# An attention, Fourier and feed-forward kernel: batch 0's first copies of the attention values move to VectorE, and three groups of instructions get other predecessors

## The chip, the cores and the metric

The kernel runs on one core of a Trainium2 chip. A core has TensorE (PE, matmuls, with PEld for the weight loads), VectorE (DVE), ScalarE (ACT), GpSimd (POOL) and SyncE (SP), which issues most of the DMA transfers. Each engine works through its own queue in order and waits for the others by semaphores. The metric is the device time of one execution in microseconds (us). The profile is of one execution of its own.

## The reference

For 8 batches, 8 heads, 576 tokens and a head size of 64: attention over keys and values that are averaged over 8 neighbours, then a two-dimensional Fourier transform of which the real part is added, a normalisation, and a feed-forward layer of 512 to 2048 to 512.

```python
k_p = k.reshape(B, H, Sp, pool, D).mean(axis=3)          # Sp = 72
v_p = v.reshape(B, H, Sp, pool, D).mean(axis=3)
scores = scale * np.matmul(q, k_p.transpose(0, 1, 3, 2))
attn = softmax(scores)                                    # exp, sum, divide
x = np.matmul(attn, v_p)                                  # to (B, S, 512)
...
u = x + np.real(np.fft.fft(np.fft.fft(x, axis=1), axis=2))
un = (u - mean(u)) / np.sqrt(var(u) + 1e-06)
out = u + np.maximum(un @ w_ch1, 0.0) @ w_ch2
```

## The kernel before

Everything is kept transposed, channels on the partitions, tokens along the free dimension. A batch's front end (`fe(b)`, a generator that is stepped by the main loop) makes `unh` and `unl`, a high and a low part of the centred activations; the feed-forward layer (`ffn`) multiplies high by high, low by high and high by low, so that three matmuls stand for one in float32. Its loop runs over blocks of 288 or 384 tokens and in each over 8 or 16 steps `f` (128 hidden channels): 12 matmuls into `g`, a Relu on ACT (`hh`), its rest on DVE (`hl`), 12 matmuls into `acc`.

The front end of batch 0 runs alone before the first block; that of batch 1 is interleaved with the first block, those of later batches with later blocks. In `fe`: `prep_k` (sums of keys into `ks`, then `kpb`), `scores` (`psS`, maxima `mx`, exponentials `t`, division on POOL), `transposes` (`psT`, `psV`, `psR` on PE; `ah` and `R` are their copies in SBUF by ACT, `rt` the copy of the columns of `t` that stand beyond 128), and `values(g)` for four pairs of heads, in the order 3, 2, 0, 1: `psX` (`ah` by `wh`, plus `R` by `wlo`), which for g = 3 and 2 is copied into `X` and for g = 0 and 1 added to and subtracted from it on DVE. Then the Fourier transform: `tmpE` and `tmpO` are sums and differences of halves of `X`, each split into a high part (`eh`, `oh`, by ACT) and a low part (`el`, `ol`, by DVE; all four are named `f` in the profile), `xe` a row that is treated apart; `psA` takes `eh`, `el`, `xe`; `psB` takes `oh` and `ol`; `psQ`, `psP` are the second transform; `psM` the mean, `less` (L661) subtracts it, `centre` (L645, L646) makes `unh` on ACT and `unl` on DVE, once for each half of the tokens.

The weights come as float64. `load_w(n)` loads piece n (two pieces, one of each matrix, for a step) into a staging buffer `wst`; `prep_w(n)` turns it into a float32 `wd`: L196 and L198 on ACT, L201 and L202 on DVE; then the cast to the high part (`w1h`, `w2h`, L206, ACT), the low part on POOL (L207), which is written to memory (L208) and loaded again step by step as `w1low`, `w2low`. The preparation of pieces 0 to 10 stands ahead of the first block in the program, that of the others between its steps. A staging buffer is loaded anew when L202 of the piece in it is done.

The order on each engine is made by a scheduler that weighs the whole program. It is bound by data and by `tc.issue_after(x)`, which puts an instruction behind x. Two tables use it for weights: `HOLD` names for each piece what L196 stands behind, `HOLDV` what L201 stands behind; "R" is the last copy of batch 0's `R`, "E" the making of `el`, "X" the first `less` of batch 0, "z" the last `unl` of its first half. Batch 1's DVE work on scores and on sums of values stands behind "z" already. `keep_busy` puts matmuls without a use (`idle` in the profile) into gaps of PE.

Of the kernel before, what the change touches and what calls it, by code (L numbers as in the profile page):

```python
# [22 lines left out]
P = 128  # L23
NPAIR = 4
W2J = 2 * J
# [27 lines left out]
E0, O0, E1, O1 = 0, 1, 2, 3  # L53
# [2 lines left out]
BUSY = {"start": 8, "S3": 3, "S2": 7, "S0": 9, "S1": 4, "T3": 3, "T0": 6, "R": 4, "X": 10, "A": 3, "P": 6, "M": 8}  # L56

HOLD = {2: "R", 3: "R", 4: "R", 5: "R", 6: "B", 7: "B", 8: "B"}
HOLDV = {4: "E", 5: "E", 6: "X", 7: "X", 8: "X"}

EARLY = [4, 6]

# [24 lines left out]
def tile_kernel(ctx: ExitStack, tc: tile.TileContext, qt, kt, vm, vr, w1, w2, cad, cbd, mkd, out):  # L87
    nc = tc.nc
# [92 lines left out]
    def prep_w(n):  # L181
        if n >= len(pieces):
            return
        i, f, c, w, _ = pieces[n]
        cl = slice(c * P, (c + w) * P)
        if wide:
            st = staged.pop(n)
            hi = st[:, :, :, 1]
            halves = st.bitcast(U16)
            d0 = wk.tile([P, DM], I32, tag="w", bufs=7, name="wd")[:, 0:w * P]  # L190
            di = d0.rearrange("p (c m) -> p c m", m=P)
            dh = d0.bitcast(U16).rearrange("p (c m h) -> p c m h", m=P, h=2)
            d0 = d0.bitcast(F32)

            with tc.issue_after(behind[HOLD[n], 0].ins) if n in HOLD else ExitStack():
                nc.scalar.activation(hi.bitcast(F32), hi.bitcast(F32), AF.Copy, scale=REBIAS)  # L196

                nc.scalar.activation(dh[:, :, :, 0], st.bitcast(U8)[:, :, :, 3], AF.Copy, scale=1.0 / 32.0, bias=-15.5 / 32.0)  # L198

            with tc.issue_after(behind[HOLDV[n], 0].ins) if n in HOLDV else ExitStack():  # L200
                nc.vector.tensor_scalar(out=dh[:, :, :, 1], in0=halves[:, :, :, 3], scalar1=0x8000, scalar2=None, op0=ALU.bitwise_and)  # L201
            nc.vector.scalar_tensor_tensor(out=di, in0=hi, scalar=3, in1=di, op0=ALU.logical_shift_left, op1=ALU.bitwise_or)  # L202
        else:
            d0 = staged.pop(n)
        wh = high(i, f)[:, cl]
        nc.scalar.copy(out=wh, in_=d0)  # L206
        nc.gpsimd.tensor_tensor(out=d0, in0=d0, in1=raw(wh), op=ALU.subtract)  # L207
        nc.sync.dma_start(wls[i][:, f, cl], d0)  # L208
        for m in after.get(n, ()):
            load_w(m)  # L210
# [39 lines left out]
    def fe(b):  # L250
# [85 lines left out]
        def scores(gi, i):  # L336
# [10 lines left out]
            for c0, n in ((0, 3), (3, 2)):  # L347
                ps = bank(b, f"psS{b}_{g}_{c0}")
                for c in range(n):
                    r0 = SROW[c0 + c]  # L350
                    mm = nc.tensor.matmul(ps[:, c * W2J:(c + 1) * W2J], lhsT=q[:, r0:r0 + P], rhs=kpb[g % 2], start=True, stop=True)  # L351
                if b == 0 and c0:
                    keep_busy(BUSY[f"S{g}"], mm)
                pv = ps[:, 0:n * W2J].rearrange("p (c h j) -> p c h j", h=2, j=J)
# [74 lines left out]
        def values(g):  # L429
            ah, al = st["a"][g]  # L430
            wh, wl = st["w", g]
            for cl in halves:
                ps = bank(b, f"psX{b}_{g}")[:, 0:HS]
                if b in NAT:
# [5 lines left out]
                if b == 0 and g == 1 and cl.start:  # L440
                    keep_busy(BUSY["X"], last)
                if g == 3:
                    nc.scalar.copy(out=Xb[:, O0, cl], in_=ps)
                    nc.scalar.copy(out=Xb[0:1, E1, cl], in_=ps[0:1])
                elif g == 2:
                    nc.scalar.copy(out=Xb[:, O1, cl], in_=ps)
                    nc.scalar.copy(out=Xb[0:1, O0, cl], in_=ps[0:1])
                    nc.scalar.copy(out=Xb[0:1, O1, cl], in_=Xb[0:1, E1, cl])
                else:
                    e = 2 * g  # L450
                    nc.vector.tensor_tensor(out=Xb[:, e, cl], in0=ps, in1=Xb[:, e + 1, cl], op=ALU.add)
                    nc.vector.tensor_tensor(out=Xb[:, e + 1, cl], in0=ps, in1=Xb[:, e + 1, cl], op=ALU.subtract)
# [114 lines left out]
        for i, m in enumerate(shares):  # L567
            if b:
                channels(i, m, 0)
            ps, _ = channels(i, m, 1)  # L570
            if i < 2:
                parts((AB[i],), ps, 258)
            else:
# [424 lines left out]
```

## Time and profile before

| what | us |
|---|---|
| median of 3 runs | 1086.92 (1086.22 to 1087.01) |
| profiled execution | 1087.56 |
| its span, first to last instruction | 1085.6 |
| PE busy in the span | 1051.1 (97%) |
| DVE, ACT, POOL busy | 615.3, 414.0, 256.0 |

The profiled execution lies 0.64 us above the median, and 1.96 us of it lie outside the span. Times within the profile are counted from the start of the span. A busy PE may still work at half its clock; the granted clock is shown beside it. In a timeline a row may merge several instructions (x4); the figure in brackets is how long the engine stood idle before it, and for what.

### The profile page before, as it was taken

The numbers are of one execution on the slowest core, as the hardware profiler recorded it, in microseconds if no ns is written. First come the engines' busy times: TensorE is split into PE (matmuls) and PEld (weight loads), VectorE is DVE, ScalarE is ACT, GpSimd is POOL, SyncE is SP. The second block draws the span as 40 slices with busy tenths as digits, with TensorE's granted clock in tenths as the row PEclk, the third lists the DMA queues.
The fourth block names the chain that finished last, engine by engine and source line by source line (L and its number), as shares of the span: only waits on it lengthen the run. The fifth ranks groups of instructions, "written<-read, shape, count | busy, mean of one in ns | idle before, by whom it ended". The sixth has DMA issues, their size and how long they took to land.

```text
span 1085.6 us, 17737 instructions
## 1 busy us (share of the span) xinstructions
PE 1051.1 (97%) x6626; PEld 1016.3 (94%) x6626; DVE 615.3 (57%) x1233; ACT 414.0 (38%) x1083; POOL 256.0 (24%) x264
## 2 busy tenths in 40 slices
PE   8878898999999999999999999999999999999998
PEld 7667688999999999999999999999999999999997
DVE  6698877855376455656376455756467434522122
ACT  5868754443244331533243431443324422311110
POOL 6626365211240032311141032300231101300000
PEclk9889999999999999999999999999999999999999
DMA  8859876655345444444444444445435333346563
GB/s 310 257 186 319 282 259 211 201 177 159 113 120 165 131 153 138 128 141 157 136 124 148 133 150 137 139 131 160 140 106 156 97 106 120 116 129 191 163 190 100
DMA packets 91909, 175.80 MB, mean 162 GB/s; under 512 B 10160, under 2 KB 17328, under 8 KB 91568
## 3 DMA queue, kind: packets, MB, share of 16 engines
q1 hardware_dynamic: 91248, 171.71, 51.0%
q0 software_dynamic: 288, 2.66, 0.6%
q8 instruction: 52, 0.85, 0.3%
q10 hardware_dynamic: 288, 0.30, 0.1%
q14 instruction: 33, 0.27, 0.1%
HBM read 156.81 MB, written 17.83 MB: 161 GB/s over the span
## 4 chain that ended last, share of the span: by engine, by line
PE 86%; DVE 5%; ACT 3%; DMA 3%; POOL 1%; issue 1%; SPq 0%; DVEq 0%; POOLq 0%; ACTq 0%
PE g L775 35%; PE acc L759 35%; PE psX L439 3%; PE psS L351 3%; PE psA L558 2%; PE psP L601 2%; PE psB L584 1%; PE psQ L601 1%; PE psT L392 1%; DMA w2l<-wd 1%; POOL wd L207 1%; DMA w1low<-w1l 1%; ACT wd L198 1%; DMA k<-in_kt 1%; PE psR L415 1%
## 5 line engine op out<-in xcount | busy, mean ns | idle before, releaser
L779 ACT ACTIVATE hh<-g 128x384 fp32r<-128x384 f32 (+1 forms) x208 | 96.6, 464 | 338.1 <-PE g L775 318.4
L780 DVE SCALAR_TENSOR_TENSOR hl<-g,hh 128x384 fp32r<-128x384 f32 (+1 forms) x208 | 108.8, 523 | 189.1 <-ACT hh L779 184.2
L759 PE MATMUL acc<-hh,w2h 128*128 128x384 f32 (+1 forms) x832 | 187.2, 327 | 0.9 <-ACT hh L779 0.7
L759 PE MATMUL acc<-hh,w2low 128*128 128x384 f32 (+1 forms) x832 | 187.3, 327 | 0.0
L775 PE MATMUL g<-unh,w1low 128*128 128x384 f32 (+1 forms) x832 | 181.1, 331 | 4.6 <-DMA w1low<-w1l 4.6
L759 PE MATMUL acc<-hl,w2h 128*128 128x384 f32 (+1 forms) x832 | 182.2, 327 | 0.9 <-DVE hl L780 0.8
L775 PE MATMUL g<-unl,w1h 128*128 128x384 f32 (+1 forms) x832 | 178.2, 328 | 3.0 <-DVE unl L646 3.0
L775 PE MATMUL g<-unh,w1h 128*128 128x384 f32 (+1 forms) x832 | 172.4, 326 | 3.1 <-DVE hl L780 2.3
L775 PEld LDWEIGHTS g<-unh,w1low 128*128 128x128 f32 x832 | 140.1, 190 | 7.8 <-DMA w1low<-w1l 5.9
L759 PEld LDWEIGHTS acc<-hh,w2h 128*128 128x128 f32 x832 | 142.9, 188 | 2.7 <-ACT hh L779 1.8
L775 PEld LDWEIGHTS g<-unh,w1h 128*128 128x128 f32 x832 | 139.7, 189 | 4.6 <-DVE hl L780 2.8
L775 PEld LDWEIGHTS g<-unl,w1h 128*128 128x128 f32 x832 | 139.9, 189 | 4.3 <-DVE unl L646 3.7
L759 PEld LDWEIGHTS acc<-hh,w2low 128*128 128x128 f32 x832 | 143.1, 188 | 0.4 <-issue 0.4
L759 PEld LDWEIGHTS acc<-hl,w2h 128*128 128x128 f32 x832 | 141.6, 189 | 2.0 <-DVE hl L780 1.8
L371 POOL TENSOR_TENSOR t<-t,sm 128x720 f32<-128x720 f32 x32 | 47.4, 1482 | 267.4 <-DVE sm L370 247.2
L286 POOL TENSOR_TENSOR k<-k 128x288 f32<-128x288 f32 (+1 forms) x56 | 37.5, 670 | 84.7 <-DMA k<-in_kt 66.5
L638 POOL TENSOR_TENSOR U<-X,U 128x576 f32<-128x576 f32 (+1 forms) x14 | 19.2, 1375 | 120.3 <-DVE X L620 119.6
L356 DVE TENSOR_REDUCE mx<-psS 128x6 f32<-128x432 f32 x64 | 33.0, 526 | 22.9 <-PE psS L351 22.5
L351 PE MATMUL psS<-kpb,q 128*128 128x144 f32 x280 | 43.3, 291 | 1.6 <-DVE t L365 1.6
L351 PEld LDWEIGHTS psS<-kpb,q 128*128 128x128 f32 x280 | 40.1, 194 | 2.2 <-DVE t L365 1.8
L368 DVE TENSOR_REDUCE sm<-t 128x10 f32<-128x720 f32 x31 | 27.9, 901 | 13.1 <-ACT t L367 12.7
L798 POOL TENSOR_TENSOR U<-U,X 128x288 f32<-128x288 f32 x2 | 1.6, 798 | 140.9 <-DVE X L793 140.9
(218 smaller groups left out, 1466.4 us busy)
## 6 DMA issues: line engine op xcount, KB each, us to landing
w1low<-w1l SPq DMA_DIRECT2D x208, 256.0 KB, 2.7
w2low<-w2l SPq DMA_DIRECT2D x208, 256.0 KB, 2.9
wst<-in_w SPq DMA_DIRECT2D x30, 512.0 KB, 5.1
k<-in_kt SPq DMA_DIRECT2D x28, 288.0 KB, 3.1
q<-in_qt SPq DMA_DIRECT2D x28, 288.0 KB, 3.4
v<-in_vm SPq DMA_DIRECT2D x28, 256.0 KB, 2.9
out<-U SPq DMA_DIRECT2D x18, 384.0 KB, 3.5
w1l<-wd SPq DMA_DIRECT2D x16, 256.0 KB, 4.6
```

What stands on the lines that cost most here:

```text
L286: behind["k" if n == 1 and src.shape[1] == J else "v", b] = nc.gpsimd.tensor_tensor(out=out if n == 1 else src[:, :, 0:n], in0=src[:, :, 0 ...
L351: mm = nc.tensor.matmul(ps[:, c * W2J:(c + 1) * W2J], lhsT=q[:, r0:r0 + P], rhs=kpb[g % 2], start=True, stop=True)
L356: nc.vector.tensor_reduce(out=mx[:, c0:c0 + n], in_=pv, op=ALU.max, axis=AX.X, negate=(b, g) in SM)
L368: nc.vector.tensor_reduce(out=sm, in_=t, op=ALU.add, axis=AX.X)
L371: ins = nc.gpsimd.tensor_tensor(out=t, in0=t, in1=sm.unsqueeze(3).broadcast_to([P, 5, 2, J]), op=ALU.mult)
L439: last = nc.tensor.matmul(ps, lhsT=w, rhs=a, start=(i == 0), stop=(i == len(mm) - 1))
L558: last = nc.tensor.matmul(ps, lhsT=w, rhs=a, start=(n == 0), stop=(n == len(mm) - 1))
L601: last = nc.tensor.matmul(ps, lhsT=w, rhs=a, start=(i == 0), stop=(i == 6))
L759: mm = nc.tensor.matmul(acc[e], lhsT=w[:, e], rhs=h, start=(f == f0 and x == 0), stop=(f == f1 - 1 and x == 2))
L775: nc.tensor.matmul(ps, lhsT=w[:, c], rhs=x[:, ti, cl], start=(n == 0), stop=(n == 11))
L779: nc.scalar.activation(hh, ps, AF.Relu)
L780: nc.vector.scalar_tensor_tensor(out=hl, in0=ps, scalar=0.0, in1=raw(hh), op0=ALU.max, op1=ALU.subtract)
```

## The change

Four edits, with two names kept for them (`behind["psA", b]` is the last matmul of `psA`).

```diff
-HOLDV = {4: "E", 5: "E", 6: "X", 7: "X", 8: "X"}
+HOLDV = {4: "E", 5: "E", 6: "z", 7: "z", 8: "z"}
...
         wh = high(i, f)[:, cl]
-        nc.scalar.copy(out=wh, in_=d0)
+        with tc.issue_after(behind["R", 0].ins) if n < 2 else ExitStack():
+            nc.scalar.copy(out=wh, in_=d0)
...
-                    mm = nc.tensor.matmul(ps[:, c * W2J:(c + 1) * W2J], lhsT=q[:, r0:r0 + P], rhs=kpb[g % 2], start=True, stop=True)
+
+                    with tc.issue_after(behind["psA", 0].ins) if b == 1 and g == 3 and c + c0 == 0 else ExitStack():
+                        mm = nc.tensor.matmul(ps[:, c * W2J:(c + 1) * W2J], lhsT=q[:, r0:r0 + P], rhs=kpb[g % 2], start=True, stop=True)
...
+            copy = nc.scalar.copy if b else nc.vector.tensor_copy
...
                 if g == 3:
-                    nc.scalar.copy(out=Xb[:, O0, cl], in_=ps)
-                    nc.scalar.copy(out=Xb[0:1, E1, cl], in_=ps[0:1])
+                    copy(out=Xb[:, O0, cl], in_=ps)
+                    copy(out=Xb[0:1, E1, cl], in_=ps[0:1])
                 elif g == 2:
-                    nc.scalar.copy(out=Xb[:, O1, cl], in_=ps)
-                    nc.scalar.copy(out=Xb[0:1, O0, cl], in_=ps[0:1])
-                    nc.scalar.copy(out=Xb[0:1, O1, cl], in_=Xb[0:1, E1, cl])
+                    copy(out=Xb[:, O1, cl], in_=ps)
+                    copy(out=Xb[0:1, O0, cl], in_=ps[0:1])
+                    copy(out=Xb[0:1, O1, cl], in_=Xb[0:1, E1, cl])
...
-            ps, _ = channels(i, m, 1)
+            ps, behind["psA", b] = channels(i, m, 1)
```

The scheduler places other instructions anew around these, on all engines. Three places.

ACT, from the copies of `psX` of batch 0 to the copy `rt` of the second pair of heads (t0_1); before:

```order
L444 COPY X_80<-psX0_3_320 1x288
L292 COPY kpb1_76<-ks_748 64x72
L293 COPY kpb1_76<-ks_748 64x72
L446 COPY X_80<-psX0_2_325 128x288
L206 CAST w1h_68<-wd_622 128x512
L447 COPY X_80<-psX0_2_325 1x288
L446 COPY X_80<-psX0_2_331 128x288
L397 COPY ah_362<-psT0_0_364 128x512
L206 CAST w2h_69<-wd_632 128x512
L447 COPY X_80<-psX0_2_331 1x288
L379 COPY rt0_240<-t0_1_258 128x5x16
```

and now, from the same two copies of `kpb` on:

```order
L293 COPY kpb1_76<-ks_748 64x72
L294 COPY kpb1_76<-ks_748 64x72
L400 COPY ah_362<-psT0_0_364 128x512
L382 COPY rt0_240<-t0_1_258 128x5x16
L319 ACTIVATE wlo_346<-vt_337,mk_72 32x64
L317 ACTIVATE wh_345<-vs_341,mk_72 128x64 x2
L319 ACTIVATE wlo_356<-vt_337,mk_72 32x64
L400 COPY ah_376<-psT0_1_378 128x512
L412 COPY ah_362<-psV0_1_384 128x64
L317 ACTIVATE wh_355<-vs_351,mk_72 128x64 x2
L412 COPY ah_376<-psV0_1_384 128x64
L424 COPY R_361<-psV0_1_384 32x64
```

No copy into `X` is left (five of the ten stand in the first piece), the two casts of weights stand behind `R` (two rows below the last one shown), and `rt` is the second row behind the `kpb` pair instead of the eighth.

DVE, from the first `less` (into X_80 from psM0_584); wd_690, wd_700 and wd_710 are pieces 6, 7 and 8. Before:

```order
L661 TENSOR_TENSOR X_80<-U_81,psM0_584 128x4x288
L201 TENSOR_SCALAR wd_690<-wst_650 128x512
L201 TENSOR_SCALAR wd_700<-wst_660 128x512
L201 TENSOR_SCALAR wd_710<-wst_674 128x512
L202 SCALAR_TENSOR_TENSOR wd_690<-wst_650,wd_690 128x512
L646 TENSOR_TENSOR unl_84<-X_80,unh_83 128x288
L202 SCALAR_TENSOR_TENSOR wd_700<-wst_660,wd_700 128x512
L646 TENSOR_TENSOR unl_84<-X_80,unh_83 128x288
L202 SCALAR_TENSOR_TENSOR wd_710<-wst_674,wd_710 128x512
L646 TENSOR_TENSOR unl_84<-X_80,unh_83 128x288 x2
L638 TENSOR_TENSOR U_81<-X_80,U_81 128x288 x2
L356 TENSOR_REDUCE mx_755<-psS1_3_0_757 128x6
```

and now:

```order
L665 TENSOR_TENSOR X_80<-U_81,psM0_584 128x4x288
L650 TENSOR_TENSOR unl_84<-X_80,unh_83 128x288 x4
L642 TENSOR_TENSOR U_81<-X_80,U_81 128x288 x2
L201 TENSOR_SCALAR wd_690<-wst_650 128x512
L201 TENSOR_SCALAR wd_700<-wst_660 128x512
L201 TENSOR_SCALAR wd_710<-wst_674 128x512
L359 TENSOR_REDUCE mx_755<-psS1_3_0_757 128x6
L359 TENSOR_REDUCE mx_755<-psS1_3_3_763 128x4
L284 TENSOR_REDUCE vt_775<-vr1_0_746 32x64
L284 TENSOR_REDUCE vs_777<-v1_3_744 128x64
L643 TENSOR_TENSOR U_81<-X_80,U_81 128x288 x2
L202 SCALAR_TENSOR_TENSOR wd_690<-wst_650,wd_690 128x512
```

The four rows of `unl` stand directly behind `less`; the conversions of pieces 6 to 8 stand behind them, and the two rows of L202 for pieces 7 and 8 further on still, behind work of batch 1.

PE, from the last `psX` of batch 0 to the transforms; psS1_3 are batch 1's first scores. Before:

```order
L439 MATMUL psX0_1_420<-R_361,wlo_356 128x288
L230 MATMUL idle_98<-ident_73 128x128 x10
L351 MATMUL psS1_3_0_757<-kpb1_76,q1_3_742 128x144 x3
L351 MATMUL psS1_3_3_763<-kpb1_76,q1_3_742 128x144 x2
L558 MATMUL psA0_0_453<-ca_70,f_439 128x258 x4
L558 MATMUL psA0_1_458<-ca_70,f_439 128x258 x4
```

and now, from the last rows of `psA` on:

```order
L562 MATMUL psA0_0_453<-ca_70,xe_79 128x258
L562 MATMUL psA0_1_458<-ca_70,xe_79 128x258
L562 MATMUL psA0_2_463<-ca_70,xe_79 34x258
L354 MATMUL psS1_3_0_757<-kpb1_76,q1_3_742 128x144 x3
L354 MATMUL psS1_3_3_763<-kpb1_76,q1_3_742 128x144
L588 MATMUL psB0_0_495<-ca_70,f_489 128x256 x2
L588 MATMUL psB0_1_504<-ca_70,f_489 128x256 x2
L354 MATMUL psS1_3_3_763<-kpb1_76,q1_3_742 128x144
L588 MATMUL psB0_0_495<-ca_70,f_490 128x256 x2
```

Batch 1's first scores stood between the filler behind `psX` and the first `psA`; now they stand between `psA` and `psB`, their last matmul inside `psB`.

## Rows read from the trace of the kernel before

**Rows 1.** The page: busy time of each engine over the span, and the granted PE clock in 40 slices of 27 us.

```profile
PE 1051.1 (97%) x6626; PEld 1016.3 (94%) x6626; DVE 615.3 (57%) x1233; ACT 414.0 (38%) x1083; POOL 256.0 (24%) x264
PEclk9889999999999999999999999999999999999999
```

**Rows 2.** Busy time by stretch. Columns: stretch, its length, busy PE, PEld, DVE, ACT, POOL, mean granted clock, DMA share, GB/s.

```profile
64.00:72.00 8.00, 4.97 (x22) 4.18 (x23) 8.00 (x12) 3.71 (x8) 4.16 (x3) 0.81 0.63 156
72.00:80.00 8.00, 6.34 (x33) 5.88 (x32) 8.00 (x17) 7.62 (x22) 1.34 (x1) 0.76 0.87 289
80.00:94.00 14.00, 11.37 (x76) 10.02 (x75) 13.96 (x27) 12.95 (x43) 9.61 (x5) 1.00 0.92 305
...
140.00:1086.00 946.00, 935.66 (x5934) 919.63 (x5934) 504.32 (x1020) 315.41 (x822) 183.49 (x176) 1.00 0.48 147
```

**Rows 3.** The waits of PE: the first row from 0 to 64 us, the others from 64 to 140 us. Columns: total us, times, longest.

```profile
PE psV L405 <- ACT rt L379: 3.9, 2, 2.6
...
PE g L775 <- DVE unl L646: 3.0, 2, 1.5
PE g L775 <- DMA w1low<-w1l: 2.9, 3, 1.5
```

**Rows 4.** Timeline of ACT from 26 to 36 us. Columns: start, us, engine, line, operation, out<-in, shape, count.

```profile
26.20 1.41 ACT L198 ACTIVATE wd<-wst 128x512 uint16<-128x512 uint8 x2
27.47 0.38 ACT L443 COPY X<-psX 128x288 f32<-128x288 f32 x1
...
28.61 0.24 ACT L292 COPY kpb<-ks 64x72 f32<-64x72 f32 x1
...
30.68 0.57 ACT L397 COPY ah<-psT 128x512 f32<-128x512 f32 x1
...
31.96 0.25 ACT L379 COPY rt<-t 128x80 f32<-128x80 f32 x1
...
34.53 0.57 ACT L421 COPY R<-psR 32x512 f32<-32x512 f32 x1
```

**Rows 5.** Timeline of POOL: the last division of batch 0's scores.

```profile
27.04 1.38 POOL L371 TENSOR_TENSOR t<-t,sm 128x720 f32<-128x720 f32 x1
```

**Rows 6.** Timeline of PE from 32 to 47 us. A matmul in float32 stands as two passes, so x4 is two matmuls.

```profile
32.27 0.28 PE L405 MATMUL psV<-ident,rt 128*32 128x128 f32 x1 [2.64 <-ACT rt L379]
...
33.72 1.50 PE L439 MATMUL psX<-ah,wh 128*128 128x288 f32 x4
35.24 1.20 PE L439 MATMUL psX<-R,wlo 32*128 32x288 f32 x4
...
40.49 4.63 PE L230 MATMUL idle<-ident 128*128 128x128 f32 x20
44.91 1.48 PE L351 MATMUL psS<-kpb,q 128*128 128x144 f32 x10
46.14 1.69 PE L558 MATMUL psA<-ca,f 128*128 128x258 f32 x12
```

**Rows 7.** Timeline of DVE from 27 to 50 us.

```profile
27.01 2.70 DVE L202 SCALAR_TENSOR_TENSOR wd<-wst,wd 128x512 int32<-128x512 int32 x2 [0.69 <-ACT wd L198]
36.00 1.01 DVE L451 TENSOR_TENSOR X<-psX,X 128x288 f32<-128x288 f32 x2 [6.29 <-PE psX L439]
...
37.82 0.46 DVE L201 TENSOR_SCALAR wd<-wst 128x512 uint16<-128x512 uint16 x1
...
41.94 0.75 DVE L518 TENSOR_TENSOR tmpE<-X 128x574 f32<-128x574 f32 x1
...
43.53 1.69 DVE L512 TENSOR_TENSOR f<-tmpE,f 128x580 fp32r<-128x580 f32 x1
...
49.32 0.76 DVE L512 TENSOR_TENSOR f<-tmpO,f 128x576 fp32r<-128x576 f32 x1
```

**Rows 8.** Timeline of DVE from 62 to 84 us.

```profile
62.08 1.35 DVE L661 TENSOR_TENSOR X<-U,psM 128x1152 f32<-128x1152 f32 x1
...
65.33 0.68 DVE L202 SCALAR_TENSOR_TENSOR wd<-wst,wd 128x512 int32<-128x512 int32 x1
65.94 1.52 DVE L646 TENSOR_TENSOR unl<-X,unh 128x288 fp32r<-128x288 f32 x1
67.38 1.76 DVE L202 SCALAR_TENSOR_TENSOR wd<-wst,wd 128x512 int32<-128x512 int32 x1
...
69.80 1.90 DVE L638 TENSOR_TENSOR U<-X,U 128x288 f32<-128x288 f32 x2
...
72.50 0.66 DVE L283 TENSOR_REDUCE vt<-vr 32x64 f32<-32x512 f32 x1
...
76.70 1.33 DVE L661 TENSOR_TENSOR X<-U,psM 128x1152 f32<-128x1152 f32 x1
...
82.39 1.54 DVE L646 TENSOR_TENSOR unl<-X,unh 128x288 fp32r<-128x288 f32 x4
```

**Rows 9.** Timeline of POOL from 61 to 74 us: all that it does there, the low parts of pieces 6, 7 and 8.

```profile
65.83 1.31 POOL L207 TENSOR_TENSOR wd<-wd,w1h 128x512 f32<-128x512 f32 x1 [13.35 <-ACT w1h L206]
67.10 1.48 POOL L207 TENSOR_TENSOR wd<-wd,w2h 128x512 f32<-128x512 f32 x1
69.97 1.41 POOL L207 TENSOR_TENSOR wd<-wd,w1h 128x512 f32<-128x512 f32 x1 [1.39 <-issue]
```

**Rows 10.** SP's queue: the loads into the staging buffers of pieces 6 to 8.

```profile
65.11 4.43 SPq L178 DMA_DIRECT2D wst<-in_w  x3
```

## The prediction, made before the changed kernel ran

> **What bounds the kernel now.** I read the page first: PE is busy for 1051.1 of 1085.6 us, and the granted clock is below full only in the first slices [rows 1]. The table by stretch says where the rest lies: from 140 us on PE works 935.66 of 946.00 us at full clock, while from 64 to 94 it is busy for 4.97 of 8, 6.34 of 8 and 11.37 of 14 us [rows 2]. So what a change of the early part is worth is by how much earlier the stream that is dense from 140 us on can begin. From 64 to 94 us the full engine is DVE (8.00 of 8.00, 8.00 of 8.00, 13.96 of 14.00), with ACT close behind it from 72 on (7.62 of 8, 12.95 of 14) [rows 2]. The waits of PE name the places that the change touches: 2.6 us for `rt` at 32.27, two waits of 1.5 us for `unl`, and 2.9 us in all for low parts of weights [rows 3].
>
> **ACT to DVE, and the first casts behind `R`.** `t` of the last pair is ready at 27.04 + 1.38 = 28.42 [rows 5], but ACT copies it into `rt` at 31.96 only, since from 26.20 on its queue has no gap: L198, the copies of `psX`, `kpb`, two casts, `ah` [rows 4]. PE waits for it until 32.27, after 2.64 us of nothing [rows 6]. Now `kpb` follows L198 at 27.5 (0.24 us and its like, together 0.5), then `ah` (0.57, the next starts about 0.1 before its end) and `rt` at 28.5, just when `t` is there. That is 3.4 us earlier. Behind `rt`, `R` was finished at 34.53 + 0.57 = 35.1, 3.1 us later; that stretch loses the last X copies and gains a pair of `wh`, about as long, so `R` is there at 31.6. PE was free at 32.27 - 2.64 = 29.6, so `psV`, `psR` and the filler run from there instead of 32.27, and `psX` starts 1.45 us later as before (33.72 - 32.27), at 31.1. Four passes with `ah` took 35.24 - 33.72 = 1.5 us and four with `R` 1.2 [rows 6]; the new order has eight and eight: `ah` to 34.1, the first sum for DVE at 34.7, the last at 36.5 instead of 40.49.
>
> DVE becomes the pace here. Its eight additions for pairs 0 and 1 and the conversion of pieces 2 and 3 lasted from 36.00 to 41.94 with waits for `psX` among them [rows 7]. Without them: 8 of about 0.38, two L201 of 0.4 [rows 7] and two L202 of 0.6 to 0.68 [rows 8] make 5.0, so `tmpE` starts at 34.7 + 5.0 = 39.7, **2.2 us earlier**. Of PE's 4.0 us only this part is used, since `psA` needs what DVE makes from `tmpE`, and DVE has no gap from there to `ol` at 49.32 [rows 7].
>
> The copies themselves cost DVE ten instructions, bounded by 0.38 us (the same copy on ACT [rows 4]) and 0.5 (half of the pair that reads `psX` at 36.00 [rows 7]): 4 to 5 us, and half as much more if each met POOL. They fall into the gap of 6.29 us that DVE had before 36.00 [rows 7], beside L202 of pieces 0 and 1. From 27.0 on, with 3.8 for the copies and 1.3 for the two L202 taken alone, they end near 32; the first `psX` that needs a bank back from one of the later copies, the third, comes at 32.6. I take nothing; with that cover gone each us late is lost in full. The casts of pieces 0 and 1 move 2 us, and their low parts are first multiplied 35 us later: nothing.
>
> **Batch 1's first scores.** They stood for 46.14 - 44.91 = 1.2 us of PE ahead of `psA` [rows 6]. As counted above, `psA` now waits for DVE, so removing them gives nothing by itself, and in their new place PE waits for `ol` anyway (49.32 + 0.76 - 2.2 = 47.9 [rows 7], where `psA` can begin near 41.2, once `tmpE`, 0.75 long, is cast). DVE reads them only behind "z". Nothing, with 1.2 us on either side as the bounds. The filler ahead of `psA` ran for 4.63 us [rows 6], and shrinks if the clock stays up; that too is hidden.
>
> **Conversions behind `unl`.** Between the first `less` (ends 62.08 + 1.35 = 63.4) and the second (76.70) DVE works without a gap for 13.3 us [rows 8]. Three of its operations are stretched, each while POOL makes a low part [rows 9]: `unl` 1.52 where one alone takes 1.54 / 4 = 0.39, L202 1.76 against 0.68, the pair of U 1.90 against 0.77 at the price of `unl`, of the same shape [rows 8]. That is 3.3 us; 10.0 remain. In the new order `unl` stands first and must wait for the first `unh` of ACT (an estimate of 0.6: one ACT pass over this shape at 0.38 [rows 4], and the signals on both sides), one sum `vt` comes ahead of the second `less` (0.66 [rows 8]) and one L201 falls behind it (0.4). For the same work that is 10.0 + 0.6 = 10.6, plus what is stretched. Bounds: none stretched, 2.7 us earlier; all three as before, 0.6 later. The low parts of pieces 6 to 8 can only follow L202 of those pieces, which now stand late in the stretch, so at most the last two L202 run beside POOL. I take one, 1.1 us: 11.7, **1.6 us earlier**.
>
> The Trainium skill, SBUF — State Buffer, Who interferes with whom, states that a DVE instruction with two inputs in SBUF contends with a GpSimd instruction that reads SBUF, one with a single SBUF input not. The trace agrees for the first half (1.52 against 0.39 us [rows 8]). By the second half the new copies, `hl`, `t` and `less`, which read PSUM, would never be stretched, so the dearer bound of the copies would fall away and 1.1 us would be the most that the late L202 of piece 7 or 8 adds; the trace has no copy on DVE that shows it.
>
> **The sum.** 2.2 + 1.6 = 3.8 us in DVE's queue near 78 us. DVE has no gap until 94 [rows 2], so it arrives there whole. Behind it PE, ACT and the low parts wait for each other in order, and I give back nothing to 0.8; with 0.3, 3.5. Against the profiled execution 1087.56 - 3.5 = 1084.1; that one lies 0.64 above the median, so 1083.4 for the median.
>
> **The rivals.**
> *PE keeps all.* The two waits for `unl` vanish (3.0 us [rows 3]), and with PE filled the clock stays up: a mean grant of 0.81 over 4.97 busy us and of 0.76 over 6.34, each a mix of 1.2 and 2.4 GHz [rows 2], loses 0.9 and 1.5. With the 2.2 of the front this is 7.6 us: 1079.3. Against it: `hl` and the second `less`, for which PE then waits, hang on a DVE that is never idle. It decides if nothing is stretched by POOL.
> *Nothing is left.* The casts of pieces 6 to 8 (about 0.6 each) filled ACT while it waited for `g`; now they stand behind `hh` and `wh`, where ACT is busy 95% and 92% [rows 2]. Those 1.8 us come off the 2.2, and if a second L202 is stretched the DVE term goes from 1.6 to 0.5, of which ACT lets nothing pass: 1086.5.
> *Slower.* SP loads three staging buffers at 65.11 as L202 of pieces 6 to 8 end [rows 10]. In the new order `less` ends 2.2 us earlier by the front, but L202 of piece 6 stands behind 0.6 of waiting, 1.5 for `unl`, two pairs of U (1.6), L201 three times (1.2), four reductions at 0.5 to 0.66 (2.3) and ends after its own 0.7: at 61.2 + 7.9 = 69.1, 4 us later than now. The DMA share is 0.87 and 0.92 where these loads must then squeeze in [rows 2]. If the low parts, not DVE, are the pace (PE already waits 2.9 us for them [rows 3]), half to all of it lands on PE: 1089 to 1091. It decides from the point where a low part lands later than the `hl` of the step before; against it, the waits for low parts are the smaller part of the 7.3 us that PE idles from 64 to 94 [rows 2], and the third load, issued by 69.5 now [rows 10], hardly moves.
>
> **How the numbers follow.** Within 0.2% (2.2 us) of 1086.92 a measurement of this kernel can't tell a change from none. Forecast 0.58, its own range 1081.5 to 1085; PE keeps all 0.12; nothing left 0.20; slower 0.10. A tenth of the forecast's share lies within 0.2%, as does nearly all of the third and a fifth of the fourth: faster 0.65, same 0.26, slower 0.09. The bounds of the terms (2.2 with 1.2 either way, 2.7 to -0.6) and the first and third rival give 1079.3 to 1087.4 for eight times in ten.
>
> **What would show it.** In the changed kernel: no wait of PE for `rt` at the second pair, `rt` near 28.5, `R` near 31.6; the last `psX` before 37; `tmpE` near 39.7, `ol` near 47; `unl` in one run of 1.5 us near 62 and no wait of PE for it; the second `less` near 73; L202 of pieces 7 or 8 stretched beside a low part; the dense part beginning 3 to 4 us earlier. I am wrong if DVE's copies run past 33 and hold `psX`, if ACT instead of DVE has no gap from 62 to 80, or if PE's waits for `w1low` before 110 us grow beyond 5 us.

## The result, and the profile after

The changed kernel takes 1096.2 us (median of 5 runs, 1094.84 to 1101.52) against 1086.92 before (1086.22 to 1088.1): a ratio of 1.0096, 95% interval 1.007 to 1.0122. It is slower by 9.3 us by the medians and 10.4 by the ratio, where 3.5 us less were forecast, and outside the range. Its profiled execution took 1094.84 us at a span of 1093.1; of before, 1087.56 at 1085.6.

On the page PE's busy digits, in 40 slices of 27 us, show two places: the early part as before, and one low slice late, the 31st, near 820 us.

```profile
span 1093.1 us, 17718 instructions
...
PE 1051.7 (96%) x6626; PEld 1019.7 (93%) x6626; DVE 613.8 (56%) x1243; ACT 410.6 (38%) x1073; POOL 253.8 (23%) x264
...
PE   8868898999999999999999999999998999999998
...
PEclk9898999999999999999999999999999999999999
```

PE's busy time is 0.6 us above that of before [rows 1], of the 7.5 us that the span grew. The rest is time in which it stands. (The busy time is a net figure: the filler ahead of `psA` shrank from 4.63 [rows 6] to 2.50 us, while matmuls behind a stall took longer.)

**The front came out nearly as worked out.** Three timelines of the changed kernel, columns as in [rows 4]. ACT, 27 to 30 us:

```profile
27.28 0.26 ACT L382 COPY rt<-t 128x80 f32<-128x80 f32 x1
...
29.83 0.57 ACT L424 COPY R<-psR 32x512 f32<-32x512 f32 x1
```

DVE, 29 to 48 us:

```profile
29.59 0.64 DVE L452 COPY X<-X 1x288 f32<-1x288 f32 x2
32.67 0.46 DVE L455 TENSOR_TENSOR X<-psX,X 128x288 f32<-128x288 f32 x1 [2.44 <-PE psX L443]
...
38.49 2.19 DVE L522 TENSOR_TENSOR tmpE<-X 128x574 f32<-128x574 f32 x1
...
41.50 0.88 DVE L516 TENSOR_TENSOR f<-tmpE,f 128x580 fp32r<-128x580 f32 x1
...
47.15 1.19 DVE L516 TENSOR_TENSOR f<-tmpO,f 128x576 fp32r<-128x576 f32 x1 [1.32 <-PE psA L562]
```

PE, 31 to 49 us:

```profile
31.89 2.20 PE L443 MATMUL psX<-R,wlo 32*128 32x288 f32 x8
34.02 2.50 PE L231 MATMUL idle<-ident 128*128 128x128 f32 x20
41.52 2.95 PE L562 MATMUL psA<-ca,f 128*128 128x258 f32 x12 [5.00 <-ACT f L515]
...
47.71 1.25 PE L354 MATMUL psS<-kpb,q 128*128 128x144 f32 x8
48.70 0.73 PE L588 MATMUL psB<-ca,f 128*128 128x256 f32 x4
```

`rt` is there at 27.3 (31.96 before [rows 4]), `R` at 30.4, the copies end at 30.2, `tmpE` begins 3.45 us earlier than before and, stretched to 2.19 us, ends 2.0 earlier [rows 7]. Behind it `psA` runs at a granted clock of 0.50 (from 41.5 to 45 us), 2.95 us where it was 1.69 [rows 6], after 5.00 us without work, and DVE waits 1.32 us for it ahead of `ol` (47.15). `psB` gains only 1.0 us (49.69 to 48.70), the first `less` 1.2 (62.08 to 60.90).

**Then the low parts are late.** The first `unl` takes 1.56 us for all four at 62.75 and PE no longer waits for it; the second `less` stands at 73.12, 3.6 us earlier than before [rows 8]. But here are the three largest waits of PE from 64 to 140 us (total, times, longest):

```profile
PE g L779 <- DMA w1low<-w1l: 5.4, 2, 3.5
PE acc L763 <- DVE hl L784: 3.4, 1, 3.4
PE psVar L725 <- DVE t L368: 2.9, 1, 2.9
```

The path of piece 6, first on DVE (`less` has ended at 62.2), then its low part on POOL:

```profile
62.75 1.56 DVE L650 TENSOR_TENSOR unl<-X,unh 128x288 fp32r<-128x288 f32 x4 [0.50 <-ACT unh L649]
...
68.78 0.67 DVE L202 SCALAR_TENSOR_TENSOR wd<-wst,wd 128x512 int32<-128x512 int32 x1
```
```profile
70.24 1.89 POOL L208 TENSOR_TENSOR wd<-wd,w1h 128x512 f32<-128x512 f32 x1 [20.38 <-ACT w1h L207]
```

SP's queue from 69 to 80 us (the staging loads, the write of piece 6's low part, two loads of low parts):

```profile
69.52 1.87 SPq L178 DMA_DIRECT2D wst<-in_w  x3
72.16 0.33 SPq L209 DMA_DIRECT2D w1l<-wd  x1
...
78.16 0.32 SPq L218 DMA_DIRECT2D w1low<-w1l  x1
...
79.96 0.42 SPq L218 DMA_DIRECT2D w1low<-w1l  x1
```

The load that stands at 78.16 here, in the kernel before:

```profile
74.67 0.33 SPq L217 DMA_DIRECT2D w1low<-w1l  x1
```

And PE, its two waits for low parts:

```profile
82.42 1.33 PE L779 MATMUL g<-unh,w1low 128*128 128x288 f32 x4 [3.54 <-DMA w1low<-w1l]
...
85.64 1.33 PE L779 MATMUL g<-unh,w1low 128*128 128x288 f32 x4 [1.90 <-DMA w1low<-w1l]
```

Each link ends where the next begins: L202 at 69.4, the cast, POOL's low part until 72.1, its write to memory at 72.16, the load of a low part at 78.16, PE at 82.42. The link in the middle is a buffer, not data. The load at 78.16 brings the low part for the third step, which is piece 4's and was written to memory from 47.74 on. But `wd`, `w1low` and `w2low` share seven buffers (the tag "w"), and this load goes into the one that piece 6's `wd` gives back when its write has landed; SP's queue waited 2.1 us for that landing. Piece 6's own low part is loaded from 79.96 on and multiplied at 85.64. Before, POOL's low part stood at 65.83 [rows 9], the load was issued at 74.67, and PE used it at 81.78 without a wait. So PE, which now got there 2.9 us earlier (78.88), began these matmuls 0.6 us later, and the fourth step's at the same time (85.64 for 85.71). Behind the waits PE runs at a lower clock: from 80 to 100 us it is busy for 14.78 of 20 us at a mean grant of 0.74, where before it was 16.44 at 1.00.

**And a stall of its own at 820 us.** From 640 us on PE waited for nothing before. The waits of the changed kernel from 640 us on:

```profile
PE psS L354 <- DVE X L665: 2.4, 1, 2.4
PE g L779 <- DVE unl L650: 2.2, 2, 1.3
```

Busy time from 820 to 840 us, columns as in [rows 2], in the kernel before and in the changed one:

```profile
820.00:840.00 20.00, 20.00 (x123) 19.79 (x122) 13.85 (x28) 7.00 (x16) 1.44 (x1) 1.00 0.50 155
820.00:840.00 20.00, 15.45 (x76) 13.60 (x75) 16.02 (x27) 8.94 (x19) 8.73 (x6) 0.91 0.38 120
```

The timeline of PE there:

```profile
819.99 0.29 PE L661 MATMUL psM<-s,avg 128*128 128x288 f32 x1
820.12 0.90 PE L354 MATMUL psS<-kpb,q 128*128 128x144 f32 x6
823.38 0.76 PE L354 MATMUL psS<-kpb,q 128*128 128x144 f32 x4 [2.35 <-DVE X L665]
824.08 2.34 PE L779 MATMUL g<-unh,w1h 128*128 128x384 f32 x8
827.34 0.61 PE L779 MATMUL g<-unl,w1h 128*128 128x384 f32 x2 [0.93 <-DVE unl L650]
829.23 1.97 PE L779 MATMUL g<-unl,w1h 128*128 128x384 f32 x5 [1.27 <-DVE unl L650]
```

Of ACT:

```profile
823.36 2.39 ACT L649 CAST unh<-X 128x576 fp32r<-128x576 f32 x4 [5.58 <-DVE X L665]
```

And of DVE:

```profile
820.12 1.95 DVE L808 TENSOR_TENSOR acc<-acc,rb 128x384 f32<-128x384 f32 x4
821.98 1.34 DVE L665 TENSOR_TENSOR X<-U,psM 128x1152 f32<-128x1152 f32 x1
...
825.81 1.48 DVE L650 TENSOR_TENSOR unl<-X,unh 128x576 fp32r<-128x576 f32 x1
```

The last modulation sum `psM` of batch 6 stands directly ahead of the block that multiplies this batch: `less` (behind the 1.95 us of the finished block's multiplications), `unh` and `unl` have to run while PE has little else. The eight matmuls at 824.08 took 2.34 us at a granted clock of 1.00 (824 to 827 us): they kept pace with the four casts of `unh`, 2.39 us. The grant fell later, to 0.51 from 829 to 832.5 us, where five matmuls took 1.97 us. Before, the same 20 us were full, since that sum stood at 808.41, with 68 feed-forward matmuls of earlier blocks behind it. The orders of the two kernels, on PE behind batch 6's last `psM`, say so (numbers at the names count tiles). Before:

```
L656 MATMUL psM_8535<-s,avg 128x288
L657 MATMUL psM_8535<-s,avg 128x288
L759 MATMUL acc_0_0_8345<-hh,w2low 128x384
L759 MATMUL acc_0_1_8346<-hh,w2low 128x384
```

and in the changed kernel:

```
L660 MATMUL psM_8535<-s,avg 128x288
L661 MATMUL psM_8535<-s,avg 128x288
L354 MATMUL psS_2_0_8609<-kpb_75,q_2_8568 128x144 x3
L354 MATMUL psS_2_3_8615<-kpb_75,q_2_8568 128x144 x2
L779 MATMUL g_3264_0_9416<-unh,w1h 128x384
```

Below, *margin* is this count: the feed-forward matmuls of earlier blocks that stand on PE behind a batch's last `psM`. For batches 2 to 7 it is 68, 261, 68, 261, **68**, 273 before and 64, 246, 27, 213, **0**, 222 after. No edit touches those batches; the scheduler, which places each instruction anew, put them later step by step.

**Where the time goes, by block ends.** The first multiplication of a finished block (DVE, `acc` by `rb`) is a milestone that both traces have. Its start against that of before, in us, with the kernels of the experiments:

| block ends before at | 130.8 | 206.0 | 404.7 | 738.1 | 823.1 | 904.0 | 978.6 | span |
|---|---|---|---|---|---|---|---|---|
| changed kernel | +1.4 | -0.8 | -2.4 | -1.1 | -3.0 | +5.0 | +7.4 | +7.5 |
| e3 copies and casts | -3.0 | -4.1 | -3.9 | -3.9 | -3.9 | -3.9 | -3.8 | -3.8 |
| e2 without the scores' tie | -1.5 | +3.3 | +3.5 | +3.5 | +3.5 | +3.5 | +3.5 | +3.5 |
| e9 one filler less, conversion as before | -3.0 | -1.3 | -1.6 | -1.8 | -1.8 | -1.8 | -1.8 | -1.8 |
| e5 whole change, one filler less | -2.0 | +4.8 | +5.0 | +5.0 | +5.0 | +5.0 | +5.0 | +5.0 |
| e7 before, batch 6 late | -0.5 | -0.2 | -0.2 | -0.2 | -4.5 | +7.1 | +8.5 | +8.5 |

Where the margins are those of before (e2, e3, e5, e9) nothing changes after 206 us to within 0.7 us. Where they are not, the numbers from 404.7 to 904 flatter the kernel: it is "earlier" because front-end work of the next batches was put off (12 matmuls of it in the changed kernel at 404.7, 9 at 738 and 823, 19 at 904). At 130.8 the changed kernel, e2 and e5 have nine such matmuls more behind them than the kernel before, e9 has five. At 206 and from 978.6 on the orders of all these kernels have as many behind them as that of before, and there the rows compare like work.

So the changed kernel's profiled execution is 0.8 us ahead of the kernel before at 206 us, and loses 8.2 from there to 978.6, as much as e7 (8.7), in which batches 6 and 7 alone are late. At 206 us e5, the same kernel but for one filler matmul, is 5.6 us behind it. That is more than the two profiled executions lie off their medians (1.4 below and 1.0 above).

### The profile page after: what moved, and what is told of

It reads as the page before. It is cut to its first block, busy times and chain, and to the rows that moved or that the text cites. A ratio compares the mean times of both kernels' runs of the same rounds, so it can differ in the third digit from the quotient of the medians.

```text
span 1093.1 us, 17718 instructions
## 1 busy us (share of the span) xinstructions
PE 1051.7 (96%) x6626; PEld 1019.7 (93%) x6626; DVE 613.8 (56%) x1243; ACT 410.6 (38%) x1073; POOL 253.8 (23%) x264
## 4 chain that ended last, share of the span: by engine, by line
PE 86%; DVE 6%; DMA 5%; ACT 2%; POOL 1%; issue 1%; SPq 0%; DVEq 0%; ACTq 0%; POOLq 0%
PE acc L763 35%; PE g L779 35%; PE psX L443 3%; PE psS L354 3%; DMA wst<-in_w 3%; PE psA L562 2%; PE psP L605 2%; PE psB L588 1%; PE psQ L605 1%; PE psT L395 1%; DMA w2l<-wd 1%; DVE wd L202 1%; PE psR L418 1%; DMA w1l<-wd 0%; DMA rb<-in_vm 0%
## 5 line engine op out<-in xcount | busy, mean ns | idle before, releaser
L779 PE MATMUL g<-unh,w1low 128*128 128x384 f32 (+1 forms) x832 | 178.4, 330 | 7.7 <-DMA w1low<-w1l 7.7
L779 PE MATMUL g<-unh,w1h 128*128 128x384 f32 (+1 forms) x832 | 177.7, 329 | 0.7 <-ACT unh L649 0.7
L370 ACT ACTIVATE t<-t 128x720 f32<-128x720 f32 x31 | 24.9, 803 | 39.3 <-DVE t L368 39.0
```

Source lines behind the costliest of these rows:

```text
L370: nc.scalar.activation(t, t, AF.Exp, scale=1.0 / 64.0)
L779: nc.tensor.matmul(ps, lhsT=w[:, c], rhs=x[:, ti, cl], start=(n == 0), stop=(n == 11))
```

## Experiments

Theory A was: the late place of batch 6 costs the whole. Rival B: the late low parts near 82 us cost it. One filler matmul more or less at the front turned out to move all later batches, and so to switch the one cause with hardly another edit. Ratios are against the kernel before on the same chip.

| run | median us | before us | ratio, 95% interval | margins of batches 2, 4, 6 |
|---|---|---|---|---|
| e1 late places pinned | 1100.22 | 1086.61 | 1.0122 (1.0102 to 1.0141) | 72, 72, 72 |
| e2 without scores' tie | 1090.76 | 1086.61 | 1.0032 (1.0018 to 1.0045) | 68, 68, 68 |
| e3 copies and casts | 1084.48 | 1086.61 | 0.9977 (0.9965 to 0.999) | 68, 68, 68 |
| e4 copies only | 1099.45 | 1086.61 | 1.0117 (1.0097 to 1.0137) | 34, 6, 0 |
| e5 whole, one filler less | 1091.72 | 1087.26 | 1.0047 (1.0031 to 1.0063) | 68, 68, 68 |
| e6 copies and casts, late | 1099.14 | 1087.26 | 1.0128 (1.0105 to 1.0151) | 40, 6, 0 |
| e7 before, batch 6 late | 1096.34 | 1087.26 | 1.01 (1.0071 to 1.0128) | 68, 68, 0 |
| e8 pieces 7, 8 behind z | 1088.35 | 1087.26 | 1.0018 (1.0002 to 1.0033) | 67, 69, 68 |
| e9 as e5, conversion as before | 1086.27 | 1088.03 | 0.9991 (0.9975 to 1.0008) | 67, 69, 68 |
| e10 copies and tie | 1084.86 | 1088.03 | 0.9969 (0.9955 to 0.9982) | 68, 68, 68 |
| e11 casts only | 1087.14 | 1088.03 | 0.9987 (0.9972 to 1.0002) | 68, 68, 68 |

**e1: the later places forced back.** `p` is the step at which the last `psM` of batch `q` was written.

```diff
+   tied = [m for q, (p, m) in pin.items() if q > 1 and n == 0 and step == p + 10]
+   with tc.issue_after(tied[-1].ins) if tied else ExitStack():
        nc.tensor.matmul(ps, lhsT=w[:, c], rhs=x[:, ti, cl], ...)
```

> The whole change, with one thing held: for every batch from 2 on, the first gate matmul of the feed-forward step that is issued ten steps after the batch's last modulation sum (psM) is ordered behind that sum. The place of batches 2 to 7 among the feed-forward matmuls then stands within 15 matmuls of the kernel before (72, 246, 72, 246, 72, 273 matmuls between a batch's last psM and its first block, against 68, 261, 68, 261, 68, 273 before and 64, 246, 27, 213, 0, 222 in the changed kernel). The work before 100 us is that of the changed kernel. Theory A (the late place of batch 6, whose last psM stands directly ahead of its block near 820 us, costs the 8 us there; the early part gives about 0 to 1.2 us): 1085 to 1088 us, no wait of PE for X or unl after 800 us, PE row at 820 to 840 us full (20 of 20 us at granted clock 1.00). Rival B (the late low parts near 82 to 92 us and the half clock there cost it, the later batches' places only show it late): 1093 us or more.

It was not faster than the changed kernel (1.0122 against 1.0096, the intervals overlap). The waits for X and `unl` at 820 are gone, but PE's order alone was forced; DVE and ACT stayed late, and PE waits at batches 4 and 6 for what `psM` reads (at batch 4, at 562.85 and 563.97, as long as here):

```profile
817.75 0.40 PE L660 MATMUL psM<-s,avg 128*128 128x288 f32 x1 [2.03 <-ACT s L636]
818.87 0.40 PE L661 MATMUL psM<-s,avg 128*128 128x288 f32 x1 [0.72 <-DVE s L637]
```

So the time doesn't tell A from B, but the block ends say where it was lost: against the kernel before it stands at +1.2 us at 488.4 and +8.1 at 573.5, at +6.5 at 738.1 and +13.2 at 823.1, that is nearly all at batches 4 and 6. A late batch is late on all its engines, and a tie on one of them only changes what it waits for.

**e2: without the scores' tie.** Against the changed kernel:

```diff
-   with tc.issue_after(behind["psA", 0].ins) if b == 1 and g == 3 and c + c0 == 0 else ExitStack():
        mm = nc.tensor.matmul(ps[:, c * W2J:(c + 1) * W2J], ...)
```

> The change without the tie of batch 1's first scores to psA: copies on VectorE, casts of pieces 0 and 1 behind R, conversion of pieces 6 to 8 behind the low parts stay. With it alone left out, the places of batches 2 to 7 are those of the kernel before (68, 261, 68, 261, 68, 273). Theory A: 1084 to 1088 us, no wait near 820 us, while w1low waits near 82 to 86 us stay (about 5 us in sum). Rival B: 1093 us or more. Rival C (the tie itself gives something at 36 to 46 us): psA would start more than 1 us later than the 41.5 us of the changed kernel.

Neither theory had it right: 1090.8. There is no wait of PE after 640 us at all, so this kernel has a cost that the late places don't explain, 4.2 us by the medians, where the change cost 9.3. The low parts are late as in the changed kernel, and here are the three largest waits of PE from 64 to 140 us:

```profile
PE g L777 <- DMA w1low<-w1l: 5.7, 2, 2.9
PE acc L761 <- DVE hl L782: 3.5, 1, 3.5
PE psVar L741 <- DVE X L738: 2.1, 1, 2.1
```

**e3: copies and casts alone.** Against e2:

```diff
-HOLDV = {4: "E", 5: "E", 6: "z", 7: "z", 8: "z"}
+HOLDV = {4: "E", 5: "E", 6: "X", 7: "X", 8: "X"}
```

> Only the copies on VectorE and the casts of pieces 0 and 1 behind R; scores and conversion are as before, and so are the places of batches 2 to 7. It prices the front part alone. By the prediction's own steps it would give 2.2 us at tmpE, by the changed kernel's trace only 1.2 us at the first less run, and less at the end: 1085 to 1087 us by theory A, with L202 of piece 6 near 63 us, wst issues near 65 us and w1low waits of PE of 3 to 5 us in sum as before. Against the run without the scores' tie it says what the conversion behind the low parts gives or costs: below it by 1 us or more if the late low parts cost, above it by 1 us or more if the earlier low runs give.

Faster than before, by 0.23%, and more than expected. Against e2, which differs from it only by the conversion of pieces 6 to 8 behind "z", it is 6 us less (0.9977 against 1.0032). Its loads stand early again; the timeline of SP, 60 to 80 us:

```profile
63.12 4.43 SPq L178 DMA_DIRECT2D wst<-in_w  x3
...
73.34 0.33 SPq L218 DMA_DIRECT2D w1low<-w1l  x1
```

and PE waits 1.6 us for low parts from 64 to 140 us instead of 5.7. It waits 3.0 us for `unl`, as before [rows 3]; by this pair that wait, which the conversion's move takes away, is the cheaper one.

**e4: the copies alone.** Against the kernel before (and the five copies by `copy`):

```diff
+            copy = nc.scalar.copy if b else nc.vector.tensor_copy
```

> Only the five copies of batch 0 on VectorE. Alone it moves the later batches as far as the whole change does (34, 211, 6, 213, 0, 222 matmuls between last psM and block), with conversion, scores and casts as before, so the low parts near 65 to 90 us are not late. Theory A: 1091 to 1097 us, with PE waiting for X or unl near 820 us as in the changed kernel, and something of the same kind near 570 us (6 matmuls there). Rival B: 1085 to 1088 us, since the low parts come as before.

It is among the slowest, with the low parts as early as before and PE waiting 4.3 us from 640 us on; its waits there:

```profile
PE psS L351 <- DVE X L662: 2.7, 1, 2.7
PE g L776 <- DVE unl L647: 1.6, 2, 1.3
```

At 560 to 600 us, where batch 4 has a margin of 6, it waits for `unl` another 2.2 us. B alone can't be the cause.

**e5: the whole change, one filler matmul less.**

```diff
-BUSY = {... "R": 4, ...}
+BUSY = {... "R": 3, ...}
```

> The whole change, with three instead of four filler matmuls behind batch 0's tail columns (R). That one matmul less, 0.1 us of TensorE, is the only edit; with it the order puts batches 2 to 7 where the kernel before has them (68, 261, 68, 261, 68, 273 matmuls between a batch's last psM and its first block; the changed kernel has 64, 246, 27, 213, 0, 222). Theory A (the late places are a cost of their own, beside that of the conversion behind the low parts): about that of the run without the scores' tie, 1089 to 1092 us, no wait for X or unl near 820 us. Rival B (the scores' tie costs at 36 to 46 us, where TensorE idles 5.0 us for the cast of f): 1094 to 1098 us, as the changed kernel.

As theory A put it: 1091.7, no wait after 640 us, and the 20 us behind 820 are full again in the table of busy times:

```profile
820.00:840.00 20.00, 20.00 (x123) 19.79 (x122) 15.31 (x30) 8.42 (x20) 3.96 (x4) 1.00 0.53 170
```

Against the changed kernel it is 0.0049 less in the ratio, 5.3 us; between the two profiled executions the difference is only 2.5 us of span.

**e6: e3 with one filler matmul more.**

```diff
-BUSY = {... "T0": 6, ...}
+BUSY = {... "T0": 7, ...}
```

> Copies on VectorE and casts behind R only, which alone took 1084.5 us, with seven instead of six filler matmuls at T0. One matmul more puts batches 2 to 7 late (40, 211, 6, 213, 0, 242 between last psM and block). Theory A: 1094 to 1101 us as the copies alone (1099.5 us, margins 34, 211, 6, 213, 0, 222), with PE waiting for X or unl near 820 us. If instead the copies alone were slow because the casts of pieces 0 and 1 stood ahead of rt, ah and R on ACT: 1084 to 1087 us.

The reverse of e5. 14.7 us above e3, which gained 2 (in the ratio 0.0151, 16 us). With the late margins the same waits are back at 820 and near 575 (`unl`, 2.2 us). Of the 15.3 us between the two spans 1.4 are there by 240 us, where both have done the same work; the rest comes later.

**e7: the kernel before, with batch 6 alone late.**

```diff
-    upto = r[3] + pos - max(free[b], r[2]) + 1 if pos >= free[b] else 0
+    upto = r[3] + pos - max(free[b], r[2]) + 1 - (b == 6) * 26 if pos >= free[b] else 0
```

> The kernel before, none of the change's edits; only the second part of batch 6 (and with it batch 7) is written out 26 positions later, so that the last psM of batch 6 stands directly ahead of its block near 820 us (0 matmuls between instead of 68), all before 740 us as in the kernel before. It prices that one late place. Theory A by the changed kernel's trace (4.6 us idle, a stretch at half clock at 824 us): 1091 to 1095 us, all of the loss between 820 and 980 us. Rival: the loss is spread over all late places: 1086 to 1088 us.

1096.3, somewhat above what was expected, and by the table of block ends all of it between 738 and 979 us. At 823 us the kernel is 4.5 us "early", since PE ran feed-forward matmuls in the place of batch 6's work (13 of its matmuls are still to come); in the whole it loses 8.5 us of span. (The half clock that the expectation puts at 824 us stood in the changed kernel from 829 to 832.5.) Its busy time from 820 to 840 us, the longest wait in PE's timeline, and a gate behind it:

```profile
820.00:840.00 20.00, 15.20 (x70) 13.92 (x71) 18.34 (x30) 9.78 (x20) 8.22 (x6) 0.83 0.40 124
```
```profile
824.03 0.61 PE L656 MATMUL psM<-s,avg 128*128 128x288 f32 x1 [3.56 <-DVE X L661]
...
827.72 2.56 PE L775 MATMUL g<-unh,w1h 128*128 128x384 f32 x7
```

The price of the late place is thus shown without any edit of the change: the 4.8 us in which PE stands, and a grant of 0.50 from 824 to 830 us. It is the place of batch 6 together with that of batch 7, whose margin went from 273 to 218.

**e8: only pieces 7 and 8 behind the low parts.** Against e3, with one filler less at A so that the margins stay:

```diff
-BUSY = {... "A": 3, ...}
+BUSY = {... "A": 2, ...}
-HOLDV = {4: "E", 5: "E", 6: "X", 7: "X", 8: "X"}
+HOLDV = {4: "E", 5: "E", 6: "X", 7: "z", 8: "z"}
```

> Copies on VectorE and casts behind R; of the conversion only pieces 7 and 8 are put behind the low parts, piece 6 stays as before; two instead of three filler matmuls at A, so that batches 2 to 7 stand as before (67, 260, 69, 261, 68, 273). Without the move of pieces 7 and 8 this was 1084.5 us, with all three (beside the tie's fillers) 1090.8 us. If piece 6 is what costs (its late end holds the next weight loads and so the low parts near 82 us): 1084 to 1087 us. If pieces 7 and 8 cost as well, since they stand in SP's queue ahead of the low loads: 1088 to 1091 us.

1088.4, in the second range but below e2. So piece 6 isn't the whole of it. From 60 to 130 us PE waited 2.2 us for low parts here, but 3.9 for `hh` and 6.0 for `hl`; how the cost divides among the pieces the runs don't settle, as the intervals of e2 and e8 overlap.

**e9: e5 with the conversion as before.** Against e5:

```diff
-HOLDV = {4: "E", 5: "E", 6: "z", 7: "z", 8: "z"}
+HOLDV = {4: "E", 5: "E", 6: "X", 7: "X", 8: "X"}
```

> The whole change with one filler matmul less at R (1091.7 us, batches 2 to 7 in the places of the kernel before), and with the conversion of pieces 6 to 8 where the kernel before has it. The only difference from that run is the conversion's place; the later batches stand as before (67, 260, 69, 261, 68, 273). Theory: the late conversion puts the loads of the low parts 3.5 to 5 us later and costs about 6 us, so 1084 to 1087 us here, with w1low loads at SP near 73 us. Rival: the tie of the scores shares that cost: 1088 us or more.

1086.3, as expected: against e5 0.0056 less, 6.1 us, the same as from e2 to e3. Two pairs of kernels that differ in `HOLDV` alone give the same price, with the margins of before.

**e10: copies and tie, without the casts behind R.** Against the changed kernel, beside `HOLDV` as before:

```diff
-        with tc.issue_after(behind["R", 0].ins) if n < 2 else ExitStack():
-            nc.scalar.copy(out=wh, in_=d0)
+        nc.scalar.copy(out=wh, in_=d0)
```

> Copies on VectorE and batch 1's first scores behind psA; casts of pieces 0 and 1 and the conversion as before; batches 2 to 7 in the places of the kernel before. Prices the casts behind R: PE should again wait for rt, 2 to 4 us near 28 to 32 us. If the 2 to 4 us of the front part come from the casts: 1086 to 1089 us. If the copies alone give it (ACT freed of five copies): 1083.5 to 1085.5 us.

0.31% faster than before. The wait for `rt` that was expected didn't come, so the casts' new place isn't needed: with the copies gone from ACT, `rt` is copied at 28.49 and PE waits 0.2 us for it.

**e11: the casts alone.** Against the kernel before:

```diff
-        nc.scalar.copy(out=wh, in_=d0)
+        with tc.issue_after(behind["R", 0].ins) if n < 2 else ExitStack():
+            nc.scalar.copy(out=wh, in_=d0)
```

> Only the casts of pieces 0 and 1 behind R; copies stay on ScalarE, the rest as before, batches 2 to 7 in the places of the kernel before. If the casts are the whole of the front gain: 1083.5 to 1085.5 us, with no wait for rt. If casts and copies each give a share: 1085 to 1086.5 us. Without effect: 1086.5 to 1087.5 us.

Unclear, 0.9987 with an interval that takes in 1. PE still waits 2.18 us for `rt`, which ACT copies at 30.82: the copies of `psX` hold it.

## Why the prediction was wrong, point by point

*ACT, `rt` and `R`: right, and a little more.* 28.5 and 31.6 were worked out, 27.3 and 30.4 came. But the prediction named the two edits together; e10 and e11 show that the copies do it and the casts add nothing that can be measured.

*DVE as the pace to `tmpE`, 2.2 us: right in size.* The last sum was forecast at 36.5 and PE was done by 34.1; DVE set the pace and `tmpE` ended 2.0 us earlier. `ol` was forecast to start at 47 and end at 47.9; it started at 47.15 and ended at 48.3, 1.7 us earlier than before. What was not foreseen: DVE waited 1.32 us ahead of it for `psA`, which the lower clock had stretched. By the first `less` 1.2 us were left. In e3, without the tie, the first `less` gains 2.0, but with the tie and one filler less (e9) it gains as much, so the loss isn't shown to be the tie's.

*The copies cost nothing: right for the front* (they ended at 30.2, forecast near 32), and e3 and e10 end up 2 to 3 us faster.

*The second `less` near 73: right, and worth little in the end.* The step that fails is the sum: "it arrives there whole", because DVE has no gap from 64 to 94 us. It rests on DVE being the pace. That DVE is full doesn't make each of its instructions wanted next. In the changed kernel the lead was 1.2 us at the first `less`, 3.6 at the second, and 0.8 at 206 us instead of 3.5. Between them PE waited 5.4 us for low parts, whose loads stood behind L202 of piece 6, and 3.4 for the first `hl`, which ran at 70.92 behind L202 of all three pieces. The move takes away 3.0 us of waiting for `unl`; in the two pairs that have it as their only edit it costs about 6 us net (e3 to e2, e9 to e5).

*The rival "slower" had the direction, at a chance of 0.10.* It put the end of L202 of piece 6 at 69.1 (69.45 came), and 1089 to 1091 for the whole; e2 and e5, which have this cause without the other, took 1090.8 and 1091.7. What it weighed wrong was the link: it followed the loads into the staging buffers, and argued that the third of them "hardly moves" (it was issued by 71.4 instead of 69.5). The link that binds at 82.42 is longer: low part on POOL, write to memory (6.0 us to landing), which sets a buffer free, then the third step's load into that buffer (about 4.2). PE already waited 2.9 us for low parts [rows 3], if for the later ones at 85.71 and after, and that row was set aside as "the smaller part". Of the 7.3 us that the block ends show between e3 and e2 at most 1.5 are lost by 131 us, where e2 has done nine front-end matmuls more, the rest by 206 (block ends of e2 and e3), in further waits for low parts (2.5 us at 170.7) and `hl` (2.8 at 190.3) and at a grant of 0.92 from 165 to 210. Whether those still come from the low parts, or from the DVE work that moved with them, isn't settled.

*What no step had: the places of the later batches.* The prediction valued the change "by how much earlier the stream that is dense from 140 us on can begin", as if that stream were the same in both kernels. It isn't: batch 6's margin went from 68 to 0, in the order of the changed kernel, readable ahead of any run. By e5 it costs the changed kernel 5.3 us (2.5 by the spans); alone, 8.5 by the spans to 10.9 by the ratio (e7); and up to 16 with batch 4 (e6). By the ratios one can write the 10.4 us as front with the tie -1.0 (e9), conversion +6.1 (e9 to e5), late places +5.3 (e5 to the changed kernel). That is no test, since such steps add up whatever they hold, and e5 and e9 carry one filler less. The changed kernel's own profile divides otherwise: 0.8 us gained by 206 us, 8.2 lost from there to 978.6. So both costs are shown, each by kernels that have it without the other, but how much of the conversion's 6 us the changed kernel pays stays open.

*The front's tie and the range.* The tie was forecast as nothing, within 1.2 us either way; e9 against e3 (0.9991 against 0.9977, intervals overlap) doesn't contradict that. Its real effect was on the order: taking it out (e2) puts the later batches back, as one filler less does (e5), while the copies alone (e4) put them late without it. The range ended at 1087.4 since the one cause was given 0.10 and the other nothing.

The version that beats both kernels is the change without its edit of `HOLDV` and without one of the other two ties: e3, without that of the scores (0.9977), or e10, without that of the casts (0.9969).

## What to carry to other kernels

Where a scheduler places instructions, an edit of the first 70 us may move work 700 us later: compare the two orders over their whole length, and count for each consumer how much independent work stands between it and its last producer. A margin that falls to zero was a stall here each time, of a size that the trace of before can't show. Before moving work out of a full engine's way, follow what it feeds to its end, through memory and through the buffers that it holds until then, and ask for the slack of that chain rather than whether the engine is busy. And ask whether parts that add up to the measured sum could have failed to do so.

## What the runs showed of the hardware

In the changed kernel, at a DMA share of 0.88 (68 to 92 us), the write of 256 KB at 72.16 took 6.0 us to landing, and the loads of 256 KB at 78.16 and 79.96 reached PE 4.3 and 5.7 us later; over the whole execution the median of the 208 loads of `w1low` is 2.7 us. The Trainium skill, DMA: Bandwidth & Descriptors, Anatomy of one DMA — SWDGE (gpsimd) path, fits DMAs issued by GpSimd with about 2 us and the bytes over 436 GB/s, which would be an estimate of 2.6 us for 256 KB. These are issued by SP, so the fit is for another path; the median lies near it, the loads beside others do not, and the measurement decides here.

`tmpE`, which reads two operands in SBUF, took 2.19 us at 38.49 against 0.75 before [rows 7], while POOL worked with hardly a gap from 36.9 to 43.5; the copies from `psX` on DVE took 0.43 to 0.44 each throughout, also beside POOL. Both are as the Trainium skill, SBUF — State Buffer, Who interferes with whom, has it.

The clock made a stall dearer than its idle time. In e7, after 3.56 us of nothing at 820 to 824 us, the granted clock was 0.50 (the 1.2 GHz level) from 824 to 830 us, and seven matmuls of a gate took 2.56 us at 827.72, where in the changed kernel four of the same shape, at 814.22 and the 2.4 GHz level, took 0.86. In the changed kernel the grant was 1.00 through the 2.35 us of nothing and up to 829 us; it was 0.51 from 829 to 832.5, behind two further waits of 0.93 and 1.27 us.
